# Sums of older slots behind the last ones, four more w_in chunks and two other w_out chunks converted in the attention, and g copied quarter by quarter

## The chip, the cores and the metric

The kernel runs on 1 core of one Trainium2 chip. The metric is the device time in microseconds (us): 574.38 is the median of 3 runs of the kernel before (573.75 to 574.51).

## The reference

Three layers stand one behind the other, all in fp32 (2304 tokens, width 512):

```python
q, k = rotate(q), rotate(k)                    # (4, 8, 576, 64)
attn = softmax(q @ k.T / 8)
x = (attn @ v)                                 # -> (2304, 512)

logits = x @ phi                               # soft MoE, 32 slots = 8 experts x 4
d = softmax over tokens of logits
slot_in = d.T @ x
slot_out[e] = relu(slot_in[e] @ w1[e]) @ w2[e] # 512 -> 1024 -> 512
x = (softmax over slots of logits) @ slot_out

h = x @ w_in                                   # 512 -> 2048
out = (h * sigmoid(h)) @ w_out                 # 2048 -> 512
```

## The kernel before

**Attention.** The 32 heads are worked as 16 pairs. A pair's loop is numbered in ticks (ten to a pair), and tables of numbers at the file's head say in which tick a side task is issued. Each pair rotates q and k (POOL, DVE, ACT), multiplies scores on PE (L353, L366), takes exponentials on ACT (L357) and multiplies by v on PE (L386). In between stand the soft MoE's logits and sums of batches 0 to 2.

**Side tasks in the attention.** w_in and w_out come as 64-bit words. `narrow` turns a 128x512 chunk into fp32 in three steps: one on ACT (L134) and two on DVE (L137, L140). `W_IN_AT` gives the ticks of 12 chunks of w_in (128 rows by 512 columns). Each is loaded by SP (0.5 MB), converted and stored to DRAM as fp32 (0.25 MB), to be read again later. `W_OUT_EARLY` names four chunks of w_out that are converted there and kept. The last four chunks of w_in are left for the last MLP (`load_last`, `conv_last`).

**Tail of the attention.** The last batch's slot sums are made in two halves, h0 and h1 (`half`). Each has logits, a maximum on DVE, an exponential on ACT (L533), small transposes (`d_t`, L550, L552), a copy to SBUF on DVE (L554) and the sums `sps` on PE (`s_mm`, L561, L565). `s_b` holds the sums of older tokens. `merge` (L568) adds h0's to it. `slots` then scales and adds h1's on DVE (L574) and folds the result to 32 slots, `si`, by a product with `stack_i` on PE (L580) and copies on DVE (L581), in two rounds. `lt` is the tokens' logits transposed, needed by the combine weights.

**Layers.** `layer1` (L871) and `layer2` (L892) are the experts' two products, on streamed weights. `slot_t` transposes a group's result to `so`.

**Last MLP.** The product `so` by w_in, called g, is 32 by 2048, and the combine weights times g give the hidden values. `g_product(n)` makes a quarter of g (512 columns) as a 128x128 tile of four pieces. For n = 1 to 3 `g_copy(n, r)` puts a piece r into the operand `gs` by four copies of 32x128, of which `ACT_QUADRANTS` says which go to ACT (L1103), the rest to DVE (L1105). `hidden(j, k)` makes step k of block j: products `hps` (L1049), sigmoid and products (L1053, L1056), and a split in high and low parts `ghi` and `glo` (L1059, L1062). In block 0 it also converts and splits a chunk of w_out (`split_wo`, `split_hl`: `wo_hi` on ACT L1031, `wo_lo` on POOL L1032). Then come 18 `ops` matmuls (L1154 to L1156), six groups of three. `G_STEPS` says behind which group of the 48 x 6 a side task is issued, such as a quarter's product, its copies, or a conversion.

What sets the order: inside `manual_schedule` (all up to `gs1`) the code's own order, engine by engine. Behind it a scheduler places the instructions in a similar order. Each engine works its queue in order. Tiles are tracked as wholes here, so a reader waits for all earlier writers of its tile.

## Time and profile before

| | |
|---|---|
| median of 3 runs | 574.38 us |
| the profiled execution's own time | 573.27 us |
| its span | 571.5 us |
| PE busy | 540.4 us (95%) |
| DVE busy | 316.9 us (55%) |
| ACT busy | 307.9 us (54%) |
| POOL busy | 111.3 us (19%) |
| attention loop | to about 282 |
| tail of the attention | 282 to 300.6 |
| layers | 300.6 to 338.2 |
| passage to the last MLP | 338.2 to 346.05 |
| last MLP with w_out's conversions | 346.05 to 401.5 |
| last MLP, the rest | 401.5 to 567.7 |

Times in the rows are in us from the span's start. PE is TensorE's matmul side, PEld its weight load, DVE VectorE, ACT ScalarE, POOL GpSimd, SP the queue that issues transfers. A row's bracket tells how long the engine had been idle before it, and what it waited for. An fp32 matmul shows as two records.

### The profile page before, as it was taken

The numbers are of one execution on the slowest core, as the hardware profiler recorded it, in microseconds if no ns is written. First come the engines' busy times: TensorE is split into PE (matmuls) and PEld (weight loads), VectorE is DVE, ScalarE is ACT, GpSimd is POOL, SyncE is SP. The second block draws the span as 40 slices with busy tenths as digits, with TensorE's granted clock in tenths as the row PEclk, the third lists the DMA queues.
The fourth block names the chain that finished last, engine by engine and source line by source line (L and its number), as shares of the span: only waits on it lengthen the run. The fifth ranks groups of instructions, "written<-read, shape, count | busy, mean of one in ns | idle before, by whom it ended". The sixth has DMA issues, their size and how long they took to land.

```text
span 571.5 us, 15141 instructions
## 1 busy us (share of the span) xinstructions
PE 540.4 (95%) x6219; PEld 438.1 (77%) x6219; DVE 316.9 (55%) x841; ACT 307.9 (54%) x612; POOL 111.3 (19%) x96
## 2 busy tenths in 40 slices
...
GB/s 301 95 56 206 266 244 278 203 116 172 224 231 172 207 265 166 249 166 107 296 322 382 306 359 179 135 93 75 0 93 18 1 1 1 96 16 0 2 0 111
DMA packets 36773, 88.70 MB, mean 155 GB/s; under 512 B 10560, under 2 KB 11872, under 8 KB 34784
## 3 DMA queue, kind: packets, MB, share of 16 engines
...
q10 hardware_dynamic: 10, 0.00, 0.0%
...
## 4 chain that ended last, share of the span: by engine, by line
PE 76%; ACT 10%; DVE 5%; DMA 4%; issue 3%; POOL 1%; SPq 1%; ACTq 0%; DVEq 0%
PE u L386 10%; PE ops L1156 10%; PE ops L1154 10%; PE ops L1155 10%; PE st L353 8%; PE psmx L300 3%; PE st_r L366 3%; PE l L871 3%; PE hps L1049 3%; ACT e L357 3%; PE xps L414 3%; DMA w_out_raw<-in_w_out_dram 2%; PE psmx L316 2%; ACT relu L308 2%; PE u L380 2%
## 5 line engine op out<-in xcount | busy, mean ns | idle before, releaser
L1056 DVE TENSOR_TENSOR hps<-hps,g 128x384 f32<-128x384 f32 x96 | 49.8, 561 | 84.6 <-ACT g L1053 84.3
L1053 ACT ACTIVATE g<-hps 128x384 f32<-128x384 f32 x96 | 42.3, 490 | 82.3 <-PE hps L1049 81.9
L1154 PE MATMUL ops<-wo_hi,ghi 128*128 128x512 f32 x216 | 84.7, 392 | 0.0
L1155 PE MATMUL ops<-wo_lo,ghi 128*128 128x512 f32 x216 | 84.4, 391 | 0.0
L1156 PE MATMUL ops<-wo_hi,glo 128*128 128x512 f32 x216 | 84.3, 390 | 0.0
L321 DVE CUSTOM_DVE_ANT_0 relu<-psmx,relu 128x288 f32<-128x288 f32 x140 | 57.7, 455 | 47.1 <-ACT e L357 36.3
L357 ACT ACTIVATE e<-st 128x512 f32<-128x512 f32 (+1 forms) x128 | 76.4, 650 | 10.9 <-PE st L353 10.9
L386 PE MATMUL u<-v,e 128*64 128x65 f32 x2048 | 80.6, 225 | 0.0
L386 PEld LDWEIGHTS u<-v,e 128*64 128x64 f32 x2048 | 71.5, 139 | 6.2 <-issue 3.0
L308 ACT ACTIVATE relu<-psmx 128x576 f32<-128x576 f32 x62 | 40.1, 652 | 51.7 <-PE psmx L300 33.6
L259 POOL TENSOR_TENSOR raw<-raw,tab 128x576 f32<-128x576 f32 x29 | 41.8, 1442 | 132.8 <-DMA raw<-in_qk_dram 96.7
L1062 DVE TENSOR_TENSOR glo<-hps,ghi 128x384 fp32r<-128x384 f32 x96 | 49.4, 552 | 5.0 <-ACT ghi L1059 1.8
L1059 ACT ACTIVATE ghi<-hps 128x384 fp32r<-128x384 f32 x96 | 45.6, 494 | 10.2 <-DVE hps L1056 10.1
L1156 PEld LDWEIGHTS ops<-wo_hi,glo 128*128 128x128 f32 x216 | 40.6, 188 | 8.5
L1155 PEld LDWEIGHTS ops<-wo_lo,ghi 128*128 128x128 f32 x216 | 40.6, 188 | 7.5 <-issue 0.4
L1154 PEld LDWEIGHTS ops<-wo_hi,ghi 128*128 128x128 f32 x216 | 40.6, 188 | 7.5 <-issue 0.2
L256 POOL TENSOR_TENSOR raw<-raw,tab 128x576 f32<-128x576 f32 x29 | 42.0, 1447 | 0.0
L353 PE MATMUL st<-hi 64*128 64x256 f32 (+1 forms) x256 | 39.7, 302 | 0.0
L353 PE MATMUL st<-mq,neg_a 64*128 64x256 f32 (+1 forms) x256 | 39.1, 297 | 0.6 <-DMA mq<-m 0.6
L353 PE MATMUL st<-hi,lo 64*128 64x256 f32 (+1 forms) x256 | 38.9, 296 | 0.0
L353 PE MATMUL st<-lo,hi 64*128 64x256 f32 (+1 forms) x256 | 38.9, 296 | 0.0
L397 DVE TENSOR_SCALAR r<-u 128x4 f32<-128x4 f32 (+1 forms) x32 | 5.2, 164 | 49.7 <-PE u L388 30.1
...
## 6 DMA issues: line engine op xcount, KB each, us to landing
...
```

The costliest lines, as they stand in the source:

```text
L308: act.activation(out=r, in_=pair[:, :, 0:HS], func=ACTF.Relu)
L321: dve.tensor_tensor_reduce(out=r[:, hd], in0=t[hd], in1=r[:, hd], scale=1.0, scalar=-3.0e38, op0=ALU.add, op1=ALU.max, accum_out=mxs[p % 2 ...
L353: pe.matmul(st[:, hd, 0:n], lhsT=a, rhs=b, start=i == 0, stop=i == 3, skip_group_check=True)
L357: act.activation(out=e[:, :, 0:n], in_=st[:, :, 0:n], func=ACTF.Exp, scale=0.125)
L386: pe.matmul(u[q:q + 64, 2 * i + hd], lhsT=e[:, hd, o:o + 64], rhs=x[:, hd], start=n == 0 and i + hd == 0, stop=n == 4, skip_group_check=True)
L1053: act.activation(out=g[i], in_=t[i], func=ACTF.Sigmoid)
L1056: dve.tensor_tensor(out=t[i], in0=t[i], in1=g[i], op=ALU.mult)
L1059: act.activation(out=ghi[:, i], in_=t[i], func=ACTF.Copy)
L1062: dve.tensor_tensor(out=glo[:, i], in0=t[i], in1=ghi[:, i].bitcast(F32), op=ALU.subtract)
L1154: pe.matmul(t, lhsT=a, rhs=wo_hi[k], start=k == 0, stop=False)
L1155: pe.matmul(t, lhsT=a, rhs=wo_lo[k], start=False, stop=False)
L1156: pe.matmul(t, lhsT=b, rhs=wo_hi[k], start=False, stop=k == 15)
```

## The change

1. `W_IN_AT` gets four more ticks (33, 63, 73, 103). All 16 chunks of w_in are converted in the attention, with a fourth fp32 tile in DRAM. `load_last` and `conv_last` go, and `load_in(3)` reads that tile back behind group 9 of the last MLP. The ACT step of the conversions writes one tile of two halves in turn.
2. `W_OUT_EARLY` is (0, 1, 6, 11) in place of (3, 6, 9, 12). The conversions of w_out 0 and 1 between the layers and the last MLP go. Their split (`wo_lo`) stays on DVE and stands ahead of `gs`.
3. Tail: `x_15(1)`, the transposes of the last x, stand behind the first of h1's logits. ACT no longer scales `s_b`; instead DVE makes `ss`, the 128x32 fold matrix times the scale. `merge` moves ahead of h1's copy L554. Five matmuls on constants are added (`busy`). `slots` copies h1's sums to SBUF (half on ACT, half on DVE) and folds older and last sums in PSUM by two groups of four matmuls, with one copy to `si`. `lt`'s transposes follow, and ACT copies them. The sum `den` is made last (`total`).
4. `slot_t` copies its 128x512 half on ACT, half on DVE.
5. `ACT_QUADRANTS` is (0, 1), and the copies of g's quarters are issued piece by piece, one piece behind the second `ops` group of each step. `G_STEPS` holds the three quarters' products. The first two `ops` groups of step 0 stand ahead of the rest of g's first quarter.

The diff, cut to its core:

```diff
@@ -39,21 +39,22 @@
-W_IN_AT = (17, 27, 37, 47, 53, 67, 77, 87, 93, 107, 117, 127)
+W_IN_AT = (17, 27, 33, 37, 47, 53, 63, 67, 73, 77, 87, 93, 103, 107, 117, 127)
...
-W_OUT_EARLY = (3, 6, 9, 12)
+W_OUT_EARLY = (0, 1, 6, 11)
...
-G_STEPS = (5, 7, 16, 19, 28, 14, 23, 37, 46, 53, 58)
-ACT_QUADRANTS = (0, 1, 2)
+G_STEPS = (5, 28, 52)
+LOAD_STEP = 9
+ACT_QUADRANTS = (0, 1)
@@ -90,7 +91,7 @@
-    w_in_32 = [dram.tile([128, 4, 512 if n else 384], F32, tag=f"w_in{n}", name=f"w_in_32_{n}") for n in range(3)]
+    w_in_32 = [dram.tile([128, 4, 512 if n else 384], F32, tag=f"w_in{n}", name=f"w_in_32_{n}") for n in range(4)]
@@ -163,17 +164,13 @@
-        elif n == 1:
+        elif n % 2:
...
-    def load_last(i):
-        t = raw_in[i] = rw.tile([128, 2, 1024], U32, tag=f"raw{1 - i}", name=f"w_in_raw3_{i}")
-        sp.dma_start(out=t, in_=w_in[256 * i:256 * i + 256, 3072:4096].rearrange("(k p) f -> p k f", p=128))
@@ -536,7 +533,8 @@
-                        act.activation(out=s_b[0][64:128], in_=s_b[0][64:128], func=ACTF.Copy, scale=sc[64:128, 5:6])
+                        ps["ss"] = p_r.tile([128, 3, NSLOT], F32, tag="dh0", name="ss")[:, 0]
+                        dve.tensor_scalar(out=ps["ss"], in0=stack_i[:, 0:NSLOT], scalar1=sc[:, 5:6], scalar2=None, op0=ALU.mult)
@@ -567,25 +565,24 @@
-                def slots():
-                    acc = s_b[0]
-                    for j in range(2):
-                        w = slice(256 * j, 256 * j + 256)
-                        dve.scalar_tensor_tensor(out=acc[0:64, w], in0=acc[0:64, w], scalar=sc[0:64, 5:6], in1=ps["s"][0:64, w], op0=ALU.mult, op1=ALU.add)
-                    t2 = ps_mx.tile([128, 2, 512], F32, tag="mx", name="si_ps")
-                    for j in range(2):
-                        t = t2[:, j]
-                        for k in range(2):
-                            c0 = 256 * j + 128 * k
-                            pe.matmul(t[:, NSLOT * k:NSLOT * k + NSLOT], lhsT=acc[:, c0:c0 + 128], rhs=stack_i[:, 0:NSLOT], start=True, stop=True)
-                        dve.tensor_copy(out=si[:, 2 * j:2 * j + 2], in_=t[:, 0:64].rearrange("p (k s) -> p k s", k=2))
+                def slots(t):
+                    o = hb[1][0:64, 0:DM]
+                    act.activation(out=o[:, 0:256], in_=ps["s"][0:64, 0:256], func=ACTF.Copy)
+                    dve.tensor_copy(out=o[:, 256:512], in_=ps["s"][0:64, 256:512])
+                    for k in range(4):
+                        pe.matmul(t[:, NSLOT * k:NSLOT * k + NSLOT], lhsT=s_b[0][:, 128 * k:128 * k + 128], rhs=ps["ss"], start=k == 0, stop=False, skip_group_check=True)
+                    for k in range(4):
+                        pe.matmul(t[:, NSLOT * k:NSLOT * k + NSLOT], lhsT=o[:, 128 * k:128 * k + 128], rhs=stack_i[0:64, 0:NSLOT], start=False, stop=True, skip_group_check=True)
+                    dve.tensor_copy(out=si, in_=t[:, 0:4 * NSLOT].rearrange("p (k s) -> p k s", k=4))
+                def total():
...
-                return logits, logits2, soft, expo, keep, d_t, s_mm, slots, merge
+                return logits, logits2, soft, expo, keep, d_t, s_mm, slots, merge, total
@@ -593,7 +590,7 @@
-            words, cv = {}, {}
+            words, cv, hws = {}, {}, []
@@ -608,7 +605,9 @@
-                cv[i] = (*narrow(words.pop(i), o, wa, f"hw{i}", f"w{NWA - 3}"), keep)
+                if not hws:
+                    hws.append(wa.tile([128, 2, 512], F32, tag=f"w{NWA - 3}", name="hw_in"))
+                cv[i] = (*narrow(words.pop(i), o, None, None, hw=hws[0][:, i % 2]), keep)
@@ -650,7 +649,7 @@
-            for i in range(12):
+            for i in range(16):
@@ -823,26 +822,35 @@
-            h1[0]((0, 1, 2))
+            h1[0]((0,))
+            x_15(1)
+            h1[0]((1, 2))
...
-            x_15(1)
...
+            h0[6]()
+            h0[8]()
+            t = ps_st.tile([128, 2, 512], F32, tag="st", name="lt3_ps")
+            def busy(n):
+                for _ in range(n):
+                    pe.matmul(t[0:64, 0, 256:512], lhsT=ones, rhs=cst_sb, start=True, stop=True)
+            busy(3)
+            h1[5]()
             h1[4]()
-            h0[6]()
-            h1[5]()
-            h0[8]()
+            busy(2)
             h1[6]()
-            t = ps_st.tile([128, 2, 512], F32, tag="st", name="lt3_ps")[:, 0]
+            h1[7](t[:, 1])
             for i, (o, n) in enumerate(CHUNKS[3]):
-                pe.transpose(t[0:n, NSLOT * i:NSLOT * i + NSLOT], hb[2][0:32, o:o + n], ident[0:32, 0:32])
-            h1[7]()
-            dve.tensor_copy(out=lt[:, 15:19], in_=t[:, 0:4 * NSLOT].rearrange("p (c s) -> p c s", c=4))
-            dve.tensor_copy(out=lt[0:64, 19], in_=t[0:64, 4 * NSLOT:5 * NSLOT])
+                pe.transpose(t[0:n, 0, NSLOT * i:NSLOT * i + NSLOT], hb[2][0:32, o:o + n], ident[0:32, 0:32])
+            act.activation(out=lt[:, 15:19], in_=t[:, 0, 0:4 * NSLOT].rearrange("p (c s) -> p c s", c=4), func=ACTF.Copy)
+            act.activation(out=lt[0:64, 19], in_=t[0:64, 0, 4 * NSLOT:5 * NSLOT], func=ACTF.Copy)
+            h1[9]()
@@ -899,7 +907,8 @@
-            act.activation(out=o, in_=op[g], func=ACTF.Copy)
+            act.activation(out=o[:, 0:256], in_=op[g][:, 0:256], func=ACTF.Copy)
+            dve.tensor_copy(out=o[:, 256:512], in_=op[g][:, 256:512])
@@ -968,13 +977,10 @@
-        load_wo(0)
         load_in(0)
-        load_wo(1)
...
-        load_last(0)
@@ -990,16 +996,10 @@
-            t, h = (wa.tile([128, 2, 512], F32, tag=f"w{i}", name=n) for i, n in ((3, "wf_first"), (4, "hw_first")))
-            for k in range(2):
-                first.append((t[:, k], narrow(raw_w.pop(k), t[:, k], None, None, hw=h[:, k])))
-        first = []
...
-        for f in first[0][1]:
-            f()
@@ -1072,13 +1072,6 @@
-    def conv_last(k):
-        if k % 2 == 0:
-            halves(3, k // 2)
-        words = raw_in[k // 2][:, k % 2].rearrange("p (n t) -> p n t", t=2)
-        for f in narrow(words, w_next[3, k], wa, f"hw3_{k}", "w3"):
-            f()
@@ -1112,13 +1105,25 @@
+    ops = {}
+    def products(j, k, i, ghi, glo):
+        if k == 0:
+            ops[j, i] = ps_o.tile([128, DM], F32, tag="o", name=f"ops{j}_{i}")
+        t = ops[j, i]
+        a, b = ghi[:, 128 * i:128 * i + 128], glo[:, 128 * i:128 * i + 128]
+        pe.matmul(t, lhsT=a, rhs=wo_hi[k], start=k == 0, stop=False)
+        pe.matmul(t, lhsT=a, rhs=wo_lo[k], start=False, stop=False)
+        pe.matmul(t, lhsT=b, rhs=wo_hi[k], start=False, stop=k == 15)
...
-        (wf0, _), (wf1, n1) = first
+        for k in range(2):
+            split_hl(k, wf_early[k], dve)
@@ -1126,34 +1131,29 @@
-        hidden(*seq[0], between=lambda: (split_hl(0, wf0, dve), g_product(0)))
-        n1[0]()
+        hidden(*seq[0], between=lambda: g_product(0))
+        for i in range(2):
+            products(0, 0, i, *gt[0, 0])
         g_spread()
-        for f in n1[1:]:
-            f()
-        split_hl(1, wf1, dve)
...
-    def copies(n):
+    extra = {}
+    def put(x, f):
+        extra.setdefault(divmod(x, NI), []).append(f)
+    put(LOAD_STEP, lambda: load_in(3))
+    for n, x in enumerate(G_STEPS):
+        put(x, lambda n=n: g_product(n + 1))
         for r in range(4):
-            g_copy(n, r)
-    extra = {}
-    for x, f in zip(G_STEPS, (lambda: g_product(1), lambda: copies(1), lambda: g_product(2), lambda: copies(2), lambda: load_last(1),
-                              lambda: conv_last(0), lambda: conv_last(1), lambda: conv_last(2), lambda: conv_last(3), lambda: g_product(3), lambda: copies(3))):
-        extra.setdefault(divmod(x, 6), []).append(f)
-    ops = {}
+            put(NI * (4 * n + r + 1) + 1, lambda n=n, r=r: g_copy(n + 1, r))
...
-            if k == 0:
-                ops[j, i] = ps_o.tile([128, DM], F32, tag="o", name=f"ops{j}_{i}")
+            if (j, k, i) not in ((0, 0, 0), (0, 0, 1)):
+                products(j, k, i, ghi, glo)
             t = ops[j, i]
-            a, b = ghi[:, 128 * i:128 * i + 128], glo[:, 128 * i:128 * i + 128]
-            pe.matmul(t, lhsT=a, rhs=wo_hi[k], start=k == 0, stop=False)
-            pe.matmul(t, lhsT=a, rhs=wo_lo[k], start=False, stop=False)
-            pe.matmul(t, lhsT=b, rhs=wo_hi[k], start=False, stop=k == 15)
```

How the rows move, at three places. A row is line, operation, output<-inputs with tile numbers, size, and a count where it repeats; all are one engine's, in the order of its queue.

The first place is the tail, from h1's transposes (`dps`) to the first product of the layers. DVE before:

```order
L554 COPY dh_4862<-dps_4911 128x96
L568 SCALAR_TENSOR_TENSOR s_b_77<-sps_4902,sc,s_b_77 64x512
L574 SCALAR_TENSOR_TENSOR s_b_77<-s_b_77,sc,sps_4918 64x256 x2
L581 COPY si<-si_ps 128x64 x2
L582 TENSOR_TENSOR scs<-sc,sb 128x2
L583 TENSOR_REDUCE den<-scs 128x1
L584 SCALAR_TENSOR_TENSOR den<-den,sc,sb 128x1
L585 TENSOR_SCALAR den<-den 128x1
L586 RECIPROCAL den<-den 128x1
L844 COPY lt<-lt_ps 128x128
L845 COPY lt<-lt_ps 64x32
```

DVE now:

```order
L537 TENSOR_SCALAR ss<-cst_sb,sc 128x32
L566 SCALAR_TENSOR_TENSOR s_b_77<-sps_4920,sc,s_b_77 64x512
L552 COPY dh_4880<-dps_4934 128x96
L571 COPY last_logits<-sps_4943 64x256
L576 COPY si<-lt_ps 128x128
L579 TENSOR_TENSOR scs<-sc,sb 128x2
L580 TENSOR_REDUCE den<-scs 128x1
L581 SCALAR_TENSOR_TENSOR den<-den,sc,sb 128x1
L582 TENSOR_SCALAR den<-den 128x1
L583 RECIPROCAL den<-den 128x1
```

PE before, from the same transposes (all `sps` products but the last are left out):

```order
L550 MATMUL dps_4911<-cst_sb,last_logits 128x32 x2
L552 MATMUL dps_4911<-cst_sb,last_logits 64x32 x2
...
L565 MATMUL sps_4918<-x_4751,dh_4862 32x64 x2
L842 MATMUL lt_ps<-cst_sb,last_logits 128x32 x4
L842 MATMUL lt_ps<-cst_sb,last_logits 64x32
L580 MATMUL si_ps<-cst_sb,s_b_77 128x32 x4
L871 MATMUL l_0_0_5037<-w_653,si 32x512
```

PE now:

```order
L841 MATMUL lt_ps<-cst_sb,ones 64x256 x3
L548 MATMUL dps_4934<-cst_sb,last_logits 128x32 x2
L550 MATMUL dps_4934<-cst_sb,last_logits 64x32 x2
L841 MATMUL lt_ps<-cst_sb,ones 64x256 x2
...
L563 MATMUL sps_4943<-x_4769,dh_4880 32x64 x2
L573 MATMUL lt_ps<-ss,s_b_77 128x32 x4
L575 MATMUL lt_ps<-cst_sb,last_logits 128x32 x4
L850 MATMUL lt_ps<-cst_sb,last_logits 128x32 x4
L850 MATMUL lt_ps<-cst_sb,last_logits 64x32
L879 MATMUL l_0_0_5063<-w_654,si 32x512
```

The fold matrix `ss` and the merge (now L566) stand ahead of h1's copy `dh` on DVE, five constant products (L841) stand on PE on both sides of h1's transposes, the two rounds of scaling, product and copy have become one, and the `lt` transposes stand behind the products.

The second place is the passage from the layers to the last MLP, on DVE, from the copy of the last group's `so` to the first hidden values. Before:

```order
L908 COPY so<-otp_5334 128x4x16
L137 TENSOR_SCALAR wf_first<-hw_first 128x512
L140 SCALAR_TENSOR_TENSOR wf_first<-w_out_raw_5212,wf_first 128x512
L929 TENSOR_TENSOR gs_5343<-g_ps,gs_5343 64x128
L1056 TENSOR_TENSOR hps_0_0_5397<-hps_0_0_5397,g_0_0_5401 128x384
L1056 TENSOR_TENSOR hps_0_1_5399<-hps_0_1_5399,g_0_1_5404 128x384
L1032 TENSOR_TENSOR wo_lo_5408<-wf_first,wo_hi_5407 128x512
L1062 TENSOR_TENSOR glo_0_5396<-hps_0_0_5397,ghi_0_5395 128x384
L1062 TENSOR_TENSOR glo_0_5396<-hps_0_1_5399,ghi_0_5395 128x384
L929 TENSOR_TENSOR gs_5343<-g_all,gs_5343 64x384
L137 TENSOR_SCALAR wf_first<-hw_first 128x512
```

Now:

```order
L911 COPY o_5351<-l_1_5259 128x256
L1032 TENSOR_TENSOR wo_lo_5389<-wf_early,wo_hi_5388 128x512
L917 COPY so<-otp_5354 128x4x16
L1032 TENSOR_TENSOR wo_lo_5393<-wf_early,wo_hi_5392 128x512
L938 TENSOR_TENSOR gs_5360<-g_ps,gs_5360 64x128
L1056 TENSOR_TENSOR hps_0_0_5424<-hps_0_0_5424,g_0_0_5428 128x384
L1056 TENSOR_TENSOR hps_0_1_5426<-hps_0_1_5426,g_0_1_5431 128x384
L1062 TENSOR_TENSOR glo_0_5423<-hps_0_0_5424,ghi_0_5422 128x384
L1062 TENSOR_TENSOR glo_0_5423<-hps_0_1_5426,ghi_0_5422 128x384
L138 TENSOR_SCALAR wf_5496<-hwo_5497 128x512
```

The two conversion steps ahead of `gs` (L929, now L938) are gone, as is the split between the products `hps` and `glo`; two splits of w_out (`wo_lo`, L1032) stand around `so`.

The third place is ACT in the last MLP's first steps, from the first half quarter `gh` of g. Before:

```order
L1095 ACTIVATE gh_5536<-g_ps_5519 128x128
L1103 ACTIVATE gs_5343<-gh_5536 32x128 x2
L1103 ACTIVATE gs_5343<-gl_5537 32x128
L1103 ACTIVATE gs_5343<-gh_5536 32x128 x2
L1103 ACTIVATE gs_5343<-gl_5537 32x128
L1103 ACTIVATE gs_5343<-gh_5536 32x128 x2
L1103 ACTIVATE gs_5343<-gl_5537 32x128
L1103 ACTIVATE gs_5343<-gh_5536 32x128 x2
L1103 ACTIVATE gs_5343<-gl_5537 32x128
L1053 ACTIVATE g_3_0_5573<-hps_3_0_5571 128x384
L1053 ACTIVATE g_3_1_5580<-hps_3_1_5578 128x384
```

Now:

```order
L1088 ACTIVATE gh_5552<-g_ps_5535 128x128
L1031 ACTIVATE wo_hi_5625<-wf_5620 128x512
L1096 ACTIVATE gs_5360<-gh_5552 32x128 x2
L1053 ACTIVATE g_3_0_5582<-hps_3_0_5580 128x384
L1053 ACTIVATE g_3_1_5589<-hps_3_1_5587 128x384
L1096 ACTIVATE gs_5360<-gh_5552 32x128 x3
L1059 ACTIVATE ghi_3_5578<-hps_3_0_5580 128x384
L1096 ACTIVATE gs_5360<-gh_5552 32x128
L1059 ACTIVATE ghi_3_5578<-hps_3_1_5587 128x384
L1031 ACTIVATE wo_hi_5674<-wf_5669 128x512
L1096 ACTIVATE gs_5360<-gh_5552 32x128
L1053 ACTIVATE g_4_0_5635<-hps_4_0_5633 128x384
```

Before, twelve copies stood in a row ahead of the next step's sigmoid; now eight stand in between the sigmoids and splits of two steps, and the others of this quarter are DVE's.

## Rows read from the trace of the kernel before

**Rows 1.** The page's first line: the span.

```profile
span 571.5 us, 15141 instructions
```

**Rows 2.** Windows by stage: start:end, length, busy per engine, TensorE clock, DMA share, GB/s.

```profile
301.44:304.85 3.41, 3.41 (x20) 1.08 (x16) 0.00 (x0) 0.00 (x0) 0.00 (x0) 0.50 1.05 399
338.20:346.05 7.85, 5.06 (x82) 3.75 (x83) 4.63 (x8) 5.55 (x13) 4.37 (x3) 1.00 0.43 174
346.05:401.50 55.45, 52.84 (x312) 41.20 (x311) 44.21 (x93) 44.98 (x109) 13.15 (x9) 1.00 0.37 124
401.50:567.70 166.20, 166.16 (x746) 138.75 (x746) 78.86 (x153) 71.43 (x155) 1.29 (x1) 1.00 0.06 24
```

**Rows 3.** Windows of five attention iterations, from one first L366 to the next.

```profile
173.35:190.71 17.36, 17.19 (x293) 15.12 (x293) 11.51 (x38) 11.83 (x22) 5.56 (x4) 1.00 0.41 134
239.47:256.86 17.39, 17.22 (x294) 15.14 (x293) 9.06 (x35) 10.97 (x21) 0.00 (x0) 1.00 0.60 193
141.79:156.93 15.14, 15.00 (x278) 13.58 (x277) 9.89 (x33) 10.22 (x19) 5.57 (x4) 1.00 0.67 230
207.21:222.36 15.15, 15.00 (x277) 13.57 (x277) 9.89 (x33) 10.81 (x20) 5.56 (x4) 1.00 0.57 196
222.36:239.47 17.11, 16.43 (x293) 14.03 (x293) 11.05 (x35) 10.67 (x20) 5.56 (x4) 1.00 0.75 262
```

**Rows 4.** Timeline of the tail: start, busy, engine, line, operation, tiles, count, idle before.

```profile
294.27 0.30 PE L550 MATMUL dps<-cst_sb,last_logits 32*128 32x32 f32 x2 [0.71 <-ACT last_logits L533]
...
295.03 0.73 DVE L568 SCALAR_TENSOR_TENSOR s_b<-sps,sc,s_b 64x512 f32<-64x512 f32 x1
...
295.17 1.07 PE L561 MATMUL sps<-x,dh 128*32 128x128 f32 x16 [0.36 <-DVE dh L554]
...
296.17 0.64 PE L565 MATMUL sps<-x,dh 64*32 64x64 f32 x16
...
296.91 0.87 DVE L574 SCALAR_TENSOR_TENSOR s_b<-s_b,sc,sps 64x256 f32<-64x256 f32 x2 [1.14 <-PE sps L565]
...
298.39 0.63 PE L580 MATMUL si_ps<-cst_sb,s_b 128*128 128x32 f32 x4 [0.32 <-DVE si L581]
...
300.60 1.92 PE L871 MATMUL l<-w,si 128*32 128x512 f32 x9 [1.58 <-DVE lt L845]
```

**Rows 5.** Timeline of the passage from the layers to the last MLP.

```profile
339.43 4.37 POOL L1032 TENSOR_TENSOR wo_lo<-wf_early,wo_hi 128x512 fp32r<-128x512 f32 x3 [22.65 <-DMA w_in<-w_in]
...
340.87 1.13 PE L1118 MATMUL warm<-cst_sb 128*128 128x256 f32 x4
...
341.02 1.64 DVE L140 SCALAR_TENSOR_TENSOR wf_first<-w_out_raw,wf_first 128x512 uint32<-128x512 uint32 x1
342.69 0.29 DVE L929 TENSOR_TENSOR gs<-g_ps,gs 64x128 fp32r<-64x128 f32 x1
...
343.04 0.61 PE L1049 MATMUL hps<-cs,gs 128*128 128x384 f32 x2 [1.04 <-DVE gs L929]
...
346.08 0.48 PE L1154 MATMUL ops<-wo_hi,ghi 128*128 128x512 f32 x1
```

**Rows 6.** The longest wait of PE, 338 to 402: total, times, longest.

```profile
PE hps L1049 <- DVE glo L1062: 1.8, 3, 1.2
```

**Rows 7.** Waits of SP's queue, 300 to 402.

```profile
SPq L176 <- PE g_all L1110: 14.2, 1, 14.2
```

**Rows 8.** Groups by line and form, 346 to 402: count, busy, mean ns, idle before.

```profile
L1103 ACT ACTIVATE gs<-gl 32x128 fp32r<-32x128 f32 x12 | 3.7, 308 | 1.2 <-DVE gl L1096 1.0
...
L140 DVE SCALAR_TENSOR_TENSOR w_in<-w_in_raw,w_in 128x512 uint32<-128x512 uint32 x4 | 2.7, 684 | 0.0
...
L134 ACT ACTIVATE hw<-w_in_raw 128x512 f32<-128x512 f32 x4 | 2.7, 682 | 0.0
...
L1105 DVE CAST gs<-gl 32x128 fp32r<-32x128 f32 x12 | 2.7, 222 | 0.2
...
L137 DVE TENSOR_SCALAR w_in<-hw 128x512 uint32<-128x512 uint32 x4 | 1.7, 419 | 0.0
```

2 lines of the change are left out of this document (1 added, 1 removed).

## The prediction

> **What bounds the kernel now.** I read the windows by stage first [rows 2]. From 401.5 on PE is busy for 166.16 of 166.20 us, and the change leaves that stretch alone: its length is fixed. So the time is decided by when this stretch begins, and by the idle time of PE ahead of it. Three stages show such time. In the first part of the last MLP PE is busy for 52.84 of 55.45 us, in the passage 5.06 of 7.85. The third is a loss that busy time hides: from 301.44 to 304.85 the granted clock is 0.50, the lower of the two levels (1.2 GHz), with all 3.41 us busy. Then I read the timeline of the tail [rows 4]: the last `sps` product ends at 296.81 (296.17 and 0.64), and the layers start at 300.60, after PE has idled for 1.58 us. The timeline of the passage [rows 5] shows DVE's conversion holding `gs`, and `gs` holding `hps`. The waits [rows 6] name DVE's `glo` as the longest hold on PE in the last MLP. Last I read five iterations of the attention [rows 3], where new work is put.
>
> The sum is made against the profiled execution, 573.27 us: its span of 571.5 [rows 1] and 1.77 around it. It lies 1.11 below the median of the runs, 574.38, so I add 1.11 at the end. About 0.2% (1.15 us) is what a measurement of this kernel can tell from no change.
>
> **The attention loop: four more conversions.** Each puts one step of 0.68 on ACT and two of 0.42 and 0.68 on DVE [rows 8], 1.79 in all, and on SP a load of 0.5 MB and a store of 0.25 MB. Iterations with and without such work can be compared. The one from 173.35 holds a conversion at a tick that ends in 3, as the four new ones do, and lasts 17.36. The one from 239.47 holds none and lasts 17.39, with 2.45 less on DVE and 0.86 less on ACT [rows 3]. The one from 207.21 has a w_out conversion beside its w_in one and lasts 15.15; the one from 141.79 has only the latter and lasts 15.14. In all four PE is busy for 99% of the time, so PE covers the conversions: price 0. Were that cover gone, the price would be PE's idle time of the worst iteration. From 222.36 on it lasts 17.11 with 16.43 busy, and conversion steps stand back to back with the rotary steps on DVE at its start; that makes 0.68 each, 2.7 for four. I take 0, with bounds 0 and +2.7. A gain is excluded, since nothing is taken out there. SP's transfers have room too: the DMA share is 0.41 to 0.75 in these iterations.
>
> **The tail.** Before, 3.79 us lie between the last `sps` and the layers: two scalings on DVE (0.87), two rounds of product (0.63 each) and copy, the steps of `den`, two copies of `lt`. Now there are two half copies of the sums. They share a tile, so the second waits for the first: 0.87 by the scalings of the same size. One group of four products counts 0.63, since the older sums' group runs under the copies. Then come one copy to `si` (0.3), the transposes of `lt` (0.5) and two copies on ACT (0.5), with hand-overs 0.35. That makes 3.15 and gains 0.64; `den` is off the path.
>
> Ahead of it something is lost. PE idled 0.71 ahead of h1's transposes and 0.36 ahead of `sps` [rows 4]. Two constant products took 1.13 at the passage [rows 5], so three make 1.3 to 1.7 and two 0.9 to 1.1. They fill those gaps and run over. DVE has the merge (0.73) ahead of `dh` now, but merges while PE runs the constants. The earlier transposes of x and logits of h1 give back some 0.5 of it. I take `sps` of h1 0.35 later (bounds -0.1 and +1.0). The tail gains 0.3 (bounds: 0.8 gained, 0.4 lost).
>
> **The clock at the layers' start.** At 0.50 the 3.41 us of products take twice what they need, so 1.7 is at stake. Before the fall PE had worked 0.63 and then idled 1.58. Now no single pause there is that long: product, copy (0.3), transposes, copies (0.5), then the layers. Five constants also lie in the 4 us ahead. I take it that the clock stays up: 1.7 gained (bounds 0 and 1.7).
>
> **The layers.** `slot_t`'s copy is split on two engines, but both halves write one tile, so they run one behind the other: 0, and 0.2 either way for the two groups. SP loses 2 loads of w_out and one of w_in here, which nothing in the layers waited for.
>
> **The passage.** Before, the conversion of w_out 0 stands on DVE to 342.66, the last step stretched to 1.64 where its usual length is 0.68 [rows 5, 8]. `gs` runs at 342.69, `hps` at 343.04, the first `ops` at 346.08. Now two splits (some 0.7 each) stand around the copy of `so`. The second runs beside the 32 products of g, so `gs` waits for these and for ACT alone: `hps` at 342.0 to 342.6, 0.4 to 1.0 earlier. A split and a conversion less also stand between `hps` and `ops`. But two `ops` groups now run ahead of the rest of g's first quarter, and the second step's `hps` waits for it, so PE has less in hand. I take 0.7 gained (bounds: 1.4 gained, 0.3 lost).
>
> While POOL ran its three splits (4.37 in all), DVE's step took 1.64. The Trainium skill, "SBUF — State Buffer", section "Who interferes with whom", says that a DVE instruction with two SBUF inputs and a GpSimd one that reads SBUF exclude each other, the second waiting for all of the first. The stretched step agrees. By that rule DVE's second split could wait out a POOL split, the passage would gain nothing, and the sum would be 570.4. I keep 0.7, since POOL has two splits left in place of three and 4.63 of 7.85 us of DVE were busy.
>
> **The last MLP to 401.5.** PE idles 2.61 us here [rows 2], 1.8 of it for `glo` [rows 6]. What held DVE and ACT goes: four conversions of w_in (ACT 2.7, DVE 1.7 and 2.7 [rows 8]) and ACT's runs of twelve copies, which stood ahead of the sigmoid. Twelve copies leave ACT (3.7) for DVE (2.7). ACT falls from 44.98 to 38.6 us, DVE from 44.21 to 42.5, so PE stays the bound. SP's queue no longer waits 14.2 us for g with w_out's loads behind it [rows 7]. I leave 0.6 of the idle time for the first two steps, where the lead is small: 2.0 gained (bounds 0 and 2.4).
>
> **Sum:** 0 - 0.3 - 1.7 - 0 - 0.7 - 2.0 = -4.7. So 568.6 by the profiled execution, and 569.7 with 1.11 added. With its own bounds this case reaches from 567.4 to 571.0.
>
> **Rivals.**
>
> *The clock falls all the same.* The last sums still pass through four hand-overs, in which PE works some 1.1 of 3 us. For it: the fall before came with PE working 1.3 of 3.8 us. Against it: the constants, and the passage, where PE idled 1.04 ahead of `hps` and kept the clock at 1.00 [rows 2, 5]. The Trainium skill, "TensorE: Matmul & The Clock Gate", section "A second HAM failure mode: psum-queue depth-cycling", says that short idle times between groups of products suffice to bring the clock down; by it this case would be the likely one. No run here shows which pause decides. The time is 1.7 more: 571.4. Chance 0.28.
>
> *PE goes on waiting in the last MLP.* DVE keeps 42.5 of 55 us, gets twelve more copies, and POOL's splits (13.15 us there) can meet its steps. If only 0.3 of the 2.61 goes, and nothing of the passage's 0.7, the sum is -2.3: 572.1. Against it: the chain there went through ACT's copies and conversions, which go. Chance 0.12.
>
> *Slower: the conversions stand in the iteration's path.* DVE and ACT then delay the rotary steps and the exponentials by the whole 1.79 of each, 7.2 for four, and the sum turns to +2.5: 576.9. The point from which this decides is 4.7 / 4, about 1.2 us for each. For it: the iteration of 17.11, with 0.68 lost. Against it: the pairs of equal iterations, and that none of the new ones adds a w_out conversion. Chance 0.09.
>
> **How the numbers follow.** The forecast has a chance of 0.51, the clock's rival 0.28, the waits' 0.12, the slower one 0.09. The predicted time is the forecast's, 569.7. The range starts at the forecast's lower bound, 567.4, takes in both middle rivals, and ends at 573.6, where the waits' rival with a fallen clock would lie (573.8). Faster by over 0.2% means below 573.2: the forecast, the clock's rival and most of the waits' one, 0.84. Within 0.2%: 0.07, mostly the waits' rival with the fall. Slower: 0.09.
>
> **What would show it.** Windows of the attention as long as before, each of the new conversions included. The layers' first products some 0.3 earlier, and no stretch at 0.50 behind them. The first `ops` some 0.7 earlier against the layers' end. PE's idle time between there and the steady stretch about 0.6 in place of 2.61, with no run of copies on ACT. The prediction is wrong if the iterations with the new conversions are longer, if the stretch at 0.50 is there again, or if `hps` still waits for `glo` or `gs` for more than 1 us in all.

## The result and the profile after

The changed kernel takes 580.78 us (median of 4 runs, 578.21 to 580.85), the kernel before 574.07 beside it (4 runs, 572.37 to 574.51): ratio 1.0111, 95% interval 1.008 to 1.0142. It is slower, and 569.7 was forecast.

The page of after: the span [rows 1], then busy time, share and instructions of each engine.

```profile
span 579.1 us, 15188 instructions
PE 547.1 (94%) x6237; PEld 440.1 (76%) x6237; DVE 327.9 (57%) x852; ACT 304.7 (53%) x602; POOL 113.4 (20%) x96
```

The profiled execution took 580.85 us. Its stages against those of before (the loop is the fifteen iterations from one first L366, now L363, to the next; the passage goes from ACT's last copy in `slot_t` to the first `ops`):

| stage | before | after | difference | forecast |
|---|---|---|---|---|
| up to the first iteration's mark | 26.29 | 24.15 | -2.14 | - |
| attention loop | 246.40 | 252.79 | +6.39 | 0 |
| tail | 27.91 | 28.48 | +0.57 | -0.3 |
| layers | 37.63 | 39.28 | +1.65 | 0, and -1.7 by the clock |
| passage | 7.85 | 6.01 | -1.84 | -0.7 |
| last MLP, first ops to last | 221.58 | 224.53 | +2.95 | -2.0 |

These sum to +7.6, the difference of the spans. The start varies between 24.1 and 26.3 from run to run, whatever the kernel (24.35 in h1_before_no_const, the kernel before less one product), so its -2.14 isn't the change's. Nor is the loop the same each time: in four more runs with this very loop and no fall of the clock in it (e4_no_busy, f1_no_const, f3_late_products, f4_act1) it took 252.38 to 254.18.

Windows of after: three iterations (the second and third answer to those from 141.79 and 207.21 in [rows 3]; the first, with a conversion where one stood before, took 17.36), the stretch at the lower clock, the passage and the first 55.45 us of the last MLP [rows 2].

```profile
106.57:124.00 17.43, 17.25 (x293) 15.15 (x293) 11.75 (x38) 11.79 (x22) 5.55 (x4) 1.00 0.51 171
140.49:158.02 17.53, 15.33 (x277) 13.65 (x277) 12.60 (x33) 10.71 (x20) 6.08 (x4) 1.00 0.62 204
209.79:226.66 16.87, 15.56 (x277) 13.69 (x277) 11.70 (x34) 10.71 (x20) 6.07 (x4) 1.00 0.67 223
306.16:309.57 3.41, 3.41 (x20) 0.85 (x16) 0.00 (x0) 0.00 (x0) 0.00 (x0) 0.50 0.96 341
344.70:350.71 6.01, 4.32 (x74) 2.92 (x74) 3.19 (x8) 4.30 (x11) 2.71 (x2) 1.00 0.37 147
350.71:406.16 55.45, 51.39 (x304) 39.69 (x304) 45.42 (x95) 41.12 (x95) 16.50 (x12) 1.00 0.31 105
```

The iteration from 140.49 took 15.14 before; now it is 17.53, with 2.2 us in which PE does nothing. The stretch at 0.50 is there again. The last MLP's 55.45 us hold 51.39 us of PE, less than before.

**The loop.** The timelines of SP, POOL and DVE around that iteration:

```profile
139.40 0.33 SPq L219 DMA_DIRECT2D raw<-in_qk_dram  x1
...
148.35 1.42 POOL L256 TENSOR_TENSOR raw<-raw,tab 128x576 f32<-128x576 f32 x1 [13.54 <-DMA raw<-in_qk_dram]
...
151.19 1.96 DVE L259 TENSOR_TENSOR raw<-raw 128x576 f32<-128x576 f32 x1
153.07 1.64 DVE L138 TENSOR_SCALAR w_in<-hw_in 128x512 uint32<-128x512 uint32 x1
154.74 0.69 DVE L141 SCALAR_TENSOR_TENSOR w_in<-w_in_raw,w_in 128x512 uint32<-128x512 uint32 x1
155.35 0.45 DVE L318 CUSTOM_DVE_ANT_0 relu<-psmx,relu 128x288 f32<-128x288 f32 x1
...
156.11 1.42 DVE L265 TENSOR_TENSOR lo<-raw,hi 128x576 fp32r<-128x576 f32 x2
```

The same rows before:

```profile
139.97 0.34 SPq L222 DMA_DIRECT2D raw<-in_qk_dram  x1
...
145.78 1.43 POOL L259 TENSOR_TENSOR raw<-raw,tab 128x576 f32<-128x576 f32 x1 [11.04 <-DMA raw<-in_qk_dram]
...
151.88 0.75 DVE L262 TENSOR_TENSOR raw<-raw 128x576 f32<-128x576 f32 x1
...
153.62 1.42 DVE L268 TENSOR_TENSOR lo<-raw,hi 128x576 fp32r<-128x576 f32 x2
```

And the waits of SP's and PE's queues in the loop of after:

```profile
SPq L219 <- DVE lo L265: 23.5, 10, 4.7
...
PE psmx L297 <- DVE mx L318: 1.9, 1, 1.9
```

Against the iteration's mark (141.79 before, 140.49 now), SP issues the raw load 1.09 ahead instead of 1.82, and POOL starts on its data 7.86 behind instead of 3.99. DVE's rotary step L259 then runs beside POOL's products and takes 1.96 in place of 0.75, the added L138 takes 1.64 in place of 0.42 [rows 8], and PE's next maximum waits for DVE. In DVE's queue the two added steps stand between the rotary step L259 and `lo` (L265). `lo` is the last reader of the raw buffer, SP's raw load L219 waits for it, and there are two such buffers, so a late `lo` makes the next raw load late: the next one goes out 0.43 ahead of its mark (157.59 and 158.02), where it was 1.82 (155.11 and 156.93).

The late issue is the smaller part of POOL's delay, 0.73 of 3.87 us. The rest is the load itself: from its issue to POOL's start it is 8.95 us (139.40 and 148.35), where it was 5.81 (139.97 and 145.78). Why the load takes longer was not isolated.

**The tail.** PE's and the copies' rows of after [rows 4]:

```profile
296.03 0.75 PE L511 MATMUL lgh<-xt,phi_sb 128*32 128x320 f32 x8
...
297.56 1.51 PE L841 MATMUL lt_ps<-cst_sb,ones 128*64 128x256 f32 x6
...
299.47 1.08 PE L841 MATMUL lt_ps<-cst_sb,ones 128*64 128x256 f32 x4
...
300.48 1.07 PE L559 MATMUL sps<-x,dh 128*32 128x128 f32 x16
...
301.48 0.64 PE L563 MATMUL sps<-x,dh 64*32 64x64 f32 x16
...
302.63 0.42 DVE L571 COPY last_logits<-sps 64x256 f32<-64x256 f32 x1 [2.79 <-ACT last_logits L570]
...
305.42 1.25 PE L879 MATMUL l<-w,si 128*32 128x512 f32 x8 [0.44 <-ACT lt L852]
```

From the end of `sps` (301.48 and 0.64) to the layers it is 3.30 us, where 3.79 were: 0.49 gained of the 0.64 forecast. DVE's copy L571 stands behind ACT's, as forecast, since they share a tile. Ahead of `sps` more was lost. It starts 4.45 behind h1's last logits (300.48 and 296.03), where it was 3.22 (295.17 and 291.95): the constants and the merge stand in that way. The earlier transposes and logits give 0.28 of these 1.23 back (from h1's first logits to its last it is 3.02 us in place of 3.30), so 0.95 is lost where I took 0.35.

**The layers.** PE in layer2's first group, after and then before:

```profile
325.17 1.93 PE L900 MATMUL l<-w,ht 128*32 128x512 f32 x12
327.03 0.70 PE L1122 MATMUL warm<-cst_sb 128*128 128x256 f32 x2
327.66 7.05 PE L900 MATMUL l<-w,ht 128*32 128x512 f32 x52
```

```profile
320.30 1.94 PE L892 MATMUL l<-w,ht 128*32 128x512 f32 x16
322.17 0.70 PE L1118 MATMUL warm<-cst_sb 128*128 128x256 f32 x2
322.80 5.41 PE L892 MATMUL l<-w,ht 128*32 128x512 f32 x48
```

The constant product that the program writes ahead of g's first quarter (`dummy(1)`) runs up here, some 20 us earlier: the code's own order, said ahead of the prediction to hold up to `gs1`, doesn't hold for it in either trace. Before it stood behind 16 records, four fours; now behind 12. The products go into four quarters of 32 columns, two products (four records) to a quarter in turn, and the quarters run side by side, four records in 0.43 us. With the constant between the third quarter's products and the fourth's, the first records go by threes, and the fourth quarter's rest is left over for the end. Windows of L900 alone in after, the last full one and the one behind it:

```profile
331.10:332.80 1.70, 1.70 (x20) 0.66 (x16) 1.00 1.04 404
332.80:334.50 1.70, 1.70 (x8) 0.33 (x3) 1.00 1.05 406
```

In the second, records start one by one, 0.43 apart, four in 1.72 us (four of its eight began in the first window).

**The passage** of after [rows 5]:

```profile
346.38 0.68 DVE L1032 TENSOR_TENSOR wo_lo<-wf_early,wo_hi 128x512 fp32r<-128x512 f32 x1
...
347.98 0.29 DVE L938 TENSOR_TENSOR gs<-g_ps,gs 64x128 fp32r<-64x128 f32 x1 [0.91 <-ACT gs L937]
...
348.33 0.83 PE L1049 MATMUL hps<-cs,gs 128*128 128x384 f32 x2
...
350.71 0.50 PE L1115 MATMUL ops<-wo_hi,ghi 128*128 128x512 f32 x1 [0.75 <-ACT ghi L1059]
```

DVE's second split keeps its 0.68 and is done long before `gs`, which waits for ACT: `hps` comes 3.62 behind the start of `slot_t`'s last copy on ACT, 1.19 earlier than before, and `ops` 2.38 behind `hps` instead of 3.04.

**The last MLP.** PE's waits in its first 60 us [rows 6], and two groups by line [rows 8]:

```profile
PE hps L1049 <- DVE glo L1062: 2.9, 3, 1.5
PE ops L1115 <- ACT ghi L1059: 0.9, 2, 0.8
PE hps L1049 <- DVE gl L1089: 0.8, 1, 0.8
```

```profile
L141 DVE SCALAR_TENSOR_TENSOR wf<-w_out_raw,wf 128x512 uint32<-128x512 uint32 x12 | 8.5, 706 | 0.3
L1098 DVE CAST gs<-gl 32x128 fp32r<-32x128 f32 x24 | 8.3, 344 | 0.4
```

Twelve conversions of w_out stand here, where ten and the rest of chunk 1's stood before, and a copy on DVE takes 344 ns where it took 222.

### The profile page after: what moved, and what is told of

It is laid out like the page before. It is cut to its first block, busy times and chain, and to the rows that moved or that the text cites. A ratio compares the mean times of both kernels' runs of the same rounds, so it can differ in the third digit from the quotient of the medians.

```text
span 579.1 us, 15188 instructions
## 1 busy us (share of the span) xinstructions
PE 547.1 (94%) x6237; PEld 440.1 (76%) x6237; DVE 327.9 (57%) x852; ACT 304.7 (53%) x602; POOL 113.4 (20%) x96
## 4 chain that ended last, share of the span: by engine, by line
PE 70%; DMA 9%; DVE 9%; ACT 7%; issue 4%; SPq 0%; ACTq 0%; POOL 0%; DVEq 0%
PE ops L1115 10%; PE ops L1116 10%; PE ops L1117 10%; PE u L383 9%; PE st L350 6%; DMA raw<-in_qk_dram 3%; PE psmx L297 3%; PE l L879 3%; PE hps L1049 3%; DMA w<-in_w_dram 2%; PE u L377 2%; PE st_r L363 2%; ACT e L354 2%; PE psmx L313 2%; DMA w_out_raw<-in_w_out_dram 2%
## 5 line engine op out<-in xcount | busy, mean ns | idle before, releaser
L256 POOL TENSOR_TENSOR raw<-raw,tab 128x576 f32<-128x576 f32 x29 | 42.0, 1447 | 134.6 <-DMA raw<-in_qk_dram 111.5
L253 POOL TENSOR_TENSOR raw<-raw,tab 128x576 f32<-128x576 f32 x29 | 44.8, 1545 | 0.0
```

What stands on the lines that cost most here:

```text
L253: eng.tensor_tensor(out=r[:, i, 0, w], in0=r[:, i, 0, w], in1=tab[:, 0, w], op=ALU.mult)
```

## The experiments

The loop's length is the first number of a window over its fifteen iterations; the other stages are cut as in the table above.

**Fewer conversions (e1_w12).** Twelve chunks in the attention, the last four loaded and converted in the last MLP, where the products of g's quarters also go back to 16 and 53:

```diff
-W_IN_AT = (17, 27, 33, 37, 47, 53, 63, 67, 73, 77, 87, 93, 103, 107, 117, 127)
+W_IN_AT = (17, 27, 37, 47, 53, 67, 77, 87, 93, 107, 117, 127)
...
-G_STEPS = (5, 28, 52)
+G_STEPS = (5, 16, 53)
...
+        load_last(0)
...
+    put(28, lambda: load_last(1))
+    for k, x in enumerate((14, 23, 37, 46)):
+        put(x, lambda k=k: conv_last(k))
```

> The changed kernel with only the first part undone: 12 chunks of w_in in the attention, the last four loaded and converted in the last MLP as before (at steps 14, 23, 37 and 46 of the 48 x 6). The changed kernel's trace has 6.4 us more in the attention's iterations (2.4, 1.3 and 1.7 of it in those from the eighth, ninth and twelfth first L363). Theory A, the four chunks cost this: the iterations go back to the lengths of before within 0.2 each, and the time falls by some 6 us, less what four conversions cost in the last MLP (0 to 2): 575 to 577. Rival, the iterations are longer for another reason (the other w_out chunks' loads, or a different start): they stay long, and the time stays at 580 or rises.

579.26 us against 573.96, ratio 1.0081 (1.0051 to 1.0111). The loop is 247.07, so its loss is the added conversions'. But the time fell by 1.5 only, to above the 575 to 577 expected: in the profiled execution the last MLP went to 227.22, with a fall of the clock in it, and the layers to 40.36, with a longer one.

**Transfers alone, steps alone (e2_traffic, e3_compute).** The one leaves out the added chunks' steps on ACT and DVE: they are loaded, and the stores send an older chunk. The other leaves out their loads: the steps work on words that are there already, and the stores come at tick 133.

```diff
...
+                if i in ADDED:
...
+                    cv[i] = [lambda: None] * 3 + [store]
+                    return
```

```diff
+                if i in ADDED:
+                    words[i] = last[-1]
+                    return
...
-                cv[i] = (*narrow(words.pop(i), o, None, None, hw=hws[0][:, i % 2]), keep)
+                cv[i] = (*narrow(words.pop(i), o, None, None, hw=hws[0][:, i % 2]), (lambda: None) if i in ADDED else keep)
...
+            at(133, late_stores)
```

> The changed kernel with the four added chunks of w_in loaded and stored as there, but without their steps on ACT and DVE (the store sends an older chunk, so these columns of w_in are not the real ones). Theory A1, the traffic: the load of 0.5 MB and the stores stand beside the load of q and k (1152 KB), which lands later (8.8 us behind its issue in place of some 5.8 in the iteration from 140.5 on), so POOL's rotary steps start later and meet DVE's steps: the three long iterations stay within 0.5 of the changed kernel (17.5, 17.7, 16.9). Theory A2, the steps on ACT and DVE: the three go back to 15.1, 16.4 and 15.2. Both together: part of the way.

> The changed kernel with the four added chunks' steps on ACT and DVE, but without their loads (the steps convert the words of the chunk before once more) and with their stores put off to tick 133 (so these columns of w_in are not the real ones). Theory A1, the traffic: the iterations go back to 15.1, 16.4 and 15.2 within 0.2. Theory A2, the steps: they stay at 17.5, 17.7 and 16.9. Both together: part of the way.

One run each: 574.31 and 577.52 us. Windows over the loop of before, e2_traffic, e3_compute and after:

```profile
26.29:272.69 246.40, 241.51 (x4308) 213.53 (x4308) 153.56 (x495) 160.89 (x287) 73.68 (x53) 0.98 0.59 195
```

```profile
24.38:270.76 246.38, 241.45 (x4308) 213.37 (x4308) 156.53 (x496) 161.09 (x287) 75.93 (x54) 0.98 0.64 208
```

```profile
24.34:273.60 249.26, 242.74 (x4308) 213.84 (x4308) 159.12 (x504) 163.33 (x291) 74.61 (x54) 0.98 0.59 197
```

```profile
24.15:276.94 252.79, 243.25 (x4308) 213.93 (x4308) 163.90 (x504) 163.23 (x291) 76.97 (x54) 0.98 0.62 203
```

Transfers alone cost nothing, steps alone 2.9, both 6.4, so neither of the two theories holds alone. DVE's column shows why it is more than the sum: four conversions are 4.4 us of DVE by [rows 8], but its busy time grows by 3.0 with the transfers alone, by 5.6 with the steps alone and by 10.3 with both. The steps delay `lo` and with it the issue of the raw loads: the one for the iteration that answers to 140.49 goes out 1.10 ahead of its mark in e3_compute, 1.82 in e2_traffic. The transfers make such loads slower: from issue to POOL's start it is 7.4 to 8.5 us in six iterations of e2_traffic, at most 7.1 before. Both bring POOL's work beside DVE's, and DVE's rows stretch.

**Other places (e5_place, g1_place2, h2_13).** The new lines stand in this order; the last is in g2_mend, below, 13 in place of 33.

```diff
-W_IN_AT = (17, 27, 33, 37, 47, 53, 63, 67, 73, 77, 87, 93, 103, 107, 117, 127)
+W_IN_AT = (17, 27, 37, 47, 53, 57, 63, 67, 77, 87, 93, 97, 103, 107, 117, 127)
+W_IN_AT = (7, 17, 27, 33, 37, 47, 53, 57, 67, 77, 87, 93, 97, 107, 117, 127)
+W_IN_AT = (7, 13, 17, 27, 37, 47, 53, 57, 67, 77, 87, 93, 97, 107, 117, 127)
```

> The changed kernel with 16 chunks of w_in as there, two of the four added ones at other ticks: 57 and 97 in place of 33 and 73. These two lie in the iterations with the soft MoE's work, where PE needs 17.4 us whatever DVE does. Theory A3 (from the two runs before: the traffic alone costs 0, the steps alone 2.9, both 6.4): a step costs where DVE's queue has a rotary step ahead of it and a relu that PE waits for behind it, and a delay there frees the buffer of q and k later, so the next load and POOL's rotary steps come later too. Then the place decides: the iterations' sum falls from 252.8 to 246.5 to 248.5, and the time by 4 to 6 us, to 575 to 577. Rival, the number decides (16 chunks are more than DVE, SP and the loads carry): the sum stays above 251.

> The changed kernel with the four added conversions at ticks 7, 33, 57 and 97 in place of 33, 63, 73 and 103; at 7, 57 and 97 DVE's two steps fall at a tick that ends in 1, where no lo of the rotary step waits behind them. Place theory: what costs is DVE's steps just ahead of lo, which frees the buffer of the next raw load; then the fifteen iterations sum to 246.8 to 248.5 (246.40 before, 252.79 after, 249.97 with two of them moved). Load theory: any four conversions more on DVE cost about 1.5 each, wherever they stand: 251.5 or more.

> The kernel of g2_mend with a conversion at tick 13 in place of 33. In g2_mend the iterations 3 to 5, behind tick 33, are 0.3, 0.6 and 1.0 longer than before. Place theory: at 13, where the raw loads still run ahead, DVE's steps hold no load; iterations 3 to 5 come back to 15.9, 16.4 and 17.4, the loop to 246.9 to 248, and the time falls by 1 to 2 against g2_mend (570.4): 568.5 to 569.5. If not, the loop stays at 248.5 or more and the time at 570 or more.

e5_place: 578.77 us against 573.33 (ratio 1.0097, 1.008 to 1.0114), loop 249.97, between what the place theory (at most 248.5) and its rival (over 251) expected. g1_place2: 575.11 in one run, loop:

```profile
24.54:272.85 248.31, 242.38 (x4309) 213.91 (x4309) 159.96 (x504) 163.44 (x291) 74.84 (x53) 0.98 0.62 206
```

The same sixteen conversions cost 1.9 in place of 6.4, by their ticks alone (1.7 and 2.7 with the same ticks in g3_tail and g2_mend, below). The iteration that took 17.53 is 15.15 again, with a conversion at the ticks it always had. That is the place theory, within its bounds; what is left stands in the iterations behind tick 7 (0.8) and 33 (1.0). h2_13 missed its 568.5 to 569.5: 574.66 against 573.83 (ratio 0.9996, 0.9974 to 1.0018), loop 249.99. At 13 the loss moved into the third and fourth iterations (16.40 and 17.22, where 15.14 and 15.86 were), so the places early in the loop are not free either. How late each `lo` may come was not measured.

**The constants in the tail (e4_no_busy).**

```diff
-            busy(3)
...
-            busy(2)
```

> The changed kernel without the five constant products of the tail. In its trace they hold h1's transposes 0.65 and the products sps another 0.6 us back, and the clock falls to 0.5 behind them all the same for some 3.4 us. Theory B, they are pure delay: the layers' first product comes 1.0 to 1.3 us earlier against the start of h1's logits, the fall is as long as before, and the time falls by 1 (the weights' later release stays). Rival, they shorten the fall: without them the stretch at 0.5 is longer by 1 us or more, or starts earlier in the tail, and the time stays within 0.3.

581.89 us (580.12 to 583.12), ratio 1.013 (1.01 to 1.016). The window at the lower clock in the profiled execution, 583.12:

```profile
300.51:310.75 10.24, 9.41 (x69) 6.47 (x67) 1.47 (x7) 0.73 (x3) 0.00 (x0) 0.50 0.63 216
```

Without the constants h1's `sps` starts 3.59 behind the last logits (300.21 and 296.62), so they cost 0.86 there. But the clock is low for 10.24 us in place of 3.41, and the tail is 1.77 longer. In this execution they would pay for themselves, and they don't keep the clock up. The times don't settle it: two of the four executions have a mean granted clock of 0.982 and 0.985, no lower than after's, so the long fall isn't in them, and the intervals of the two ratios overlap.

**The fold matrix in `si`'s tile (e8_ss).**

```diff
-                        ps["ss"] = p_r.tile([128, 3, NSLOT], F32, tag="dh0", name="ss")[:, 0]
+                        ps["ss"] = si[:, 0]
```

> The changed kernel with the scaled fold matrix ss kept in the tile of si, in place of a tile of the attention's space. Theory W: the last five weight loads ahead of the layers wait for that space, with ss until the products of the older sums have read it; they were issued 2.27 ahead of the layers' start (3.75 before), and the layers took 39.3 us (37.6 before), the products of layer 2 running one by one as their weights land. Then the loads are issued some 1 us earlier and the layers take 38.0 to 38.6. Rival: the loads wait for h1's sums or something else behind them anyway, or the layers are longer for another reason: 39.3 within 0.3.

583.62 us in one run. The layers are 37.66, below the 38.0 to 38.6 expected, and for another reason: the constant stands behind 16 records again. Why it moves was not settled. The loop was 256.81, with a fall of the clock in it.

**No constant in the layers (f1_no_const; h1_before_no_const in the kernel before).**

```diff
-        dummy(1)
```

> The changed kernel without the one constant product (the first of the three on constants in the passage) that stands in the layers between the third and the fourth of the four 32-column products of layer2. Theory: behind it the fourth quarter of the array runs one product behind the other three, and at the end of that group four products run one by one: 1.72 us. Then the layers (first product to the copy of the second group's sums) go from 39.28 to about 37.6 us, and everything else stays. Rival 1, the weights come late (SP issues them 1 us later than before): 39.3 stays. Rival 2, only the constant's own time: 39.28 less 0.2 to 0.35, 39.0.

> The kernel before, without the one constant product in its layers, which stands there at a boundary of four products (1.20 us from the product ahead of it to the one behind, where 0.43 is usual). If a full-width product between 32-column products costs 0.75 at a boundary, the layers go from 37.63 to 36.9 (35.2 where the clock doesn't fall), and the time by 0.75, 572.5 against 573.2. If PE only waits there for something else that the constant covers, the layers stay at 37.6.

578.49 us in one run, and 571.62 against 573.83 for the kernel before (ratio 0.997, 0.9955 to 0.9986). PE in f1_no_const:

```profile
325.22 7.14 PE L900 MATMUL l<-w,ht 128*32 128x512 f32 x64
```

All 64 records come in fours. The layers take 35.19, less than the 37.6 expected, since in this execution the clock didn't fall there. g1_place2 and e6_act3, also without a fall there, have the constant where after has it, and take 37.59. So the constant costs 2.40, and after's 39.28 less 37.59 is the fall's price, 1.69. In the kernel before, at a boundary of four, it cost 37.63 less 36.85, 0.78. So 1.6 of the 2.40 is the fourth quarter's lone run. The weights, whose last loads SP issues 2.26 us ahead of the layers in place of 3.75, hold nothing here. The time of h1_before_no_const fell by more than these 0.78, and part of that is the clock's: its mean is 0.979 in one of 12 executions, in 15 of the 23 of the kernel before.

**The last MLP (e6_act3, e7_early, f2_row, f4_act1, f3_late_products).**

The edits in this order:

```diff
-ACT_QUADRANTS = (0, 1)
+ACT_QUADRANTS = (0, 1, 2)
```

```diff
-W_OUT_EARLY = (0, 1, 6, 11)
+W_OUT_EARLY = (0, 1, 3, 5)
```

```diff
-G_STEPS = (5, 28, 52)
+G_STEPS = (5, 16, 53)
+C_STEPS = (7, 19, 58)
...
-            put(NI * (4 * n + r + 1) + 1, lambda n=n, r=r: g_copy(n + 1, r))
+            put(C_STEPS[n], lambda n=n, r=r: g_copy(n + 1, r))
```

```diff
-ACT_QUADRANTS = (0, 1)
+ACT_QUADRANTS = (0,)
```

```diff
-        for i in range(2):
-            products(0, 0, i, *gt[0, 0])
...
-            if (j, k, i) not in ((0, 0, 0), (0, 0, 1)):
-                products(j, k, i, ghi, glo)
+            products(j, k, i, ghi, glo)
```

> The changed kernel with three of g's four quadrants copied by ACT, as before, piece by piece as in the change. In the last MLP the changed kernel needs 224.5 from the first ops to the end, 2.95 more than before, with 4.6 of waits for DVE and ACT. Theory M1, the twelve copies that went to DVE (2.7 us, and 0.5 to 0.9 more where POOL's splits run) hold glo: the stretch falls to 222.5 to 223.3. Rival M2, the denser w_out conversions of the first steps hold it: it stays at 224.5 within 0.4, or rises as ACT gets 3.7 us more.

> The changed kernel with w_out chunks 0, 1, 3 and 5 converted early in place of 0, 1, 6 and 11. Steps 2 to 5 of the last MLP then convert two chunks in place of four. Theory M2, the conversions of four steps in a row make DVE and ACT late there: from the first ops to the end 222.5 to 223.5 in place of 224.5. Rival M1, the copies of g do it: 224.5 within 0.4. The attention is as in the changed kernel.

> The changed kernel with the copies of each quarter of g in a row, behind groups 7, 19 and 58, and the products at 5, 16 and 53, as before. Theory 1: copies piece by piece write the one tile of gs between the steps, so each next hps product waits for the copies just issued; in a row the stretch from the first ops to the end goes from 224.5 to about 222.5. Theory 2: ACT and DVE are full with the conversions, and where the copies stand changes nothing: 224.5 within 0.4. Theory 3: a row of copies holds the sigmoid of the next step, worse than now: 225.5 or more.

> The changed kernel with one quadrant of the copies on ACT and three on DVE (12 copies more on DVE, 12 less on ACT). Moving 12 to ACT cost 2.7 us. Theory 1, ACT's queue holds the sigmoid and with it PE: the stretch from the first ops to the end falls from 224.5 to 223 or less. Theory 2, DVE's queue is the one that holds (PE's waits name glo and gl): 225.5 or more. Theory 3, neither: 224.5 within 0.4.

> The changed kernel with the first two groups of products behind g's first quarter again, as before. Theory 1: the two early groups stand ahead of g_all and so of step 1's hps, and the hidden values lose lead that they never make up, since ACT and DVE are nearly full; without them the stretch from the first hps to the end goes from 226.9 (2.38 and 224.53) to about 225.2 (224.62 before). Theory 2: the early groups gain what they were put there for; without them the stretch grows to 227.3 or more. Theory 3: neither, 226.9 within 0.3.

One run each: 584.51, 587.19, 583.78, 582.93 and 579.80 us; what counts is the stretch from the first `ops`, 224.53 in after. More copies on ACT: 227.21, so M1 fails. Other chunks early: 226.31, which neither theory expected. Copies in a row: 223.76, so 0.8 of the loss at most. Fewer copies on ACT: 224.48, nothing. Without the early products: 221.24, and with the 0.6 by which `ops` then starts later, 224.22 from the first `hps` against 226.91, better than the 225.2 expected. PE's waits in f3_late_products, and its window that answers to the one above:

```profile
PE hps L1049 <- DVE glo L1062: 2.8, 3, 1.4
PE g_all L1103 <- ACT gf L1085: 0.5, 1, 0.5
```

```profile
352.95:408.40 55.45, 52.58 (x312) 41.68 (x312) 45.01 (x97) 41.29 (x97) 16.76 (x12) 1.00 0.32 105
```

The early groups put `g_all` 4.01 us behind the first `hps` in place of 2.10, and with it step 1's `hps` 6.29 (354.62 and 348.33) in place of 4.69 (354.66 and 349.97). The steps then start 0.6, 0.7, 1.8 and 2.5 later against the first `hps` (steps 1 to 4): a lead once lost grows, since DVE is busy for 45 of 55 us.

**All three undone (g2_mend), with the old tail (g3_tail), and the passage alone (g4_twelve).** g2_mend takes the places of g1_place2 and leaves out `dummy(1)` and the early products; g3_tail also puts back the old `slots` and order of the tail; g4_twelve is g3_tail with twelve chunks in the attention and the quarters' products at 16 and 53, as e1_w12 has them.

```diff
-W_IN_AT = (17, 27, 33, 37, 47, 53, 63, 67, 73, 77, 87, 93, 103, 107, 117, 127)
+W_IN_AT = (7, 17, 27, 33, 37, 47, 53, 57, 67, 77, 87, 93, 97, 107, 117, 127)
...
-        dummy(1)
...
-        for i in range(2):
-            products(0, 0, i, *gt[0, 0])
...
```

> The same places, and without the constant product in the layers and without the two early groups of products. If the three findings add up: the layers 37.6 less 0.75 (the constant at a group's boundary costs 0.75), so 36.9 with a clock fall of 3.41 there and 35.2 without; from the first hps to the end 224.2; the time against before: loop +0.4 to +2, tail +0.6, layers -0.75, to the first hps -1.2, from there -0.4: 0.2% to 0.3% faster at best, 573 to 575. If they don't add up, over 576.

> The kernel of g2_mend with the tail of the attention as it was before (two scalings, two rounds, no constants). If the new tail is worth 0.6 less than the old one, as the stretch from the last mark to the layers says (28.48 against 27.91), this is 0.6 faster than g2_mend: 572.5 to 574.5. If the constants keep the clock's fall short, as the run without them said (10.24 us of fall), it is 1 to 3 us slower than g2_mend.

> The kernel before with only the passage's part of the change (w_out 0 and 1 converted in the attention, slot_t's copy on two engines, g's quarters piece by piece), the last four chunks of w_in left to the last MLP, the old tail, no early products, no constant in the layers. Expected: loop 246.4 to 247.1, tail 27.9, layers 36.9, to the first hps 3.62, from there to the end 224.2 to 225.5 (224.62 before): 1.0 to 2.5 us faster than before, 571.6 to 573. If the conversions in the last MLP cost more than 2 there, no faster.

Twelve runs each, against 573.23 (29 runs): g2_mend 570.37 us, ratio 0.9956 (0.9931 to 0.998); g3_tail 571.96, 0.9962 (0.9944 to 0.9981); g4_twelve 574.26, 1.0016 (1.0 to 1.0033). So the three findings account for the loss, and g2_mend is 0.4% faster than the kernel before, more than expected; g4_twelve is no faster, where 571.6 to 573 was expected. The traced execution of g2_mend is one of its slowest (573.53, of 568.36 to 573.81), so its stages don't show the gain. The intervals of new and old tail overlap. By its stages the new one is 0.3 longer here (28.18 and 27.91), but its mean granted clock is 0.985, the value of the executions without a fall, in 4 of 12 runs (old tail: 2 of 12; before: 2 of 29). In g4_twelve the last MLP takes 226.08 where g3_tail takes 221.61: leaving w_in's four conversions there, with the products moved for them, costs 4.5.

## Why the prediction was wrong, step by step

**The attention loop, forecast 0 (bounds 0 and +2.7), measured +6.39: the step that failed.** "In all four PE is busy for 99% of the time, so PE covers the conversions: price 0." The equal pairs of [rows 3] don't carry that. The short ones, 15.14 and 15.15, are not one with and one without: DVE has 33 instructions and 9.89 us in both, and the trace shows one conversion's two steps in each, behind `lo` (w_out's in the one from 207.21; the w_in steps named beside it fall, on DVE, into the next iteration). The long ones, 17.36 and 17.39, do compare, and the one from 173.35 even has DVE's two steps between the rotary step and `lo`:

```profile
184.72 0.75 DVE L262 TENSOR_TENSOR raw<-raw 128x576 f32<-128x576 f32 x1
185.38 0.42 DVE L137 TENSOR_SCALAR w_in<-hw 128x512 uint32<-128x512 uint32 x1
185.84 0.69 DVE L140 SCALAR_TENSOR_TENSOR w_in<-w_in_raw,w_in 128x512 uint32<-128x512 uint32 x1
...
187.73 1.41 DVE L268 TENSOR_TENSOR lo<-raw,hi 128x576 fp32r<-128x576 f32 x2
```

But there PE has 17.2 us of work with or without a conversion. No pair told what the same order costs in a shorter iteration, or in two in a row: the one ahead of 140.49 has it too and keeps its length (16.49, and 16.47 before), but its next raw load goes out late, and the one from 140.49, with an added conversion of its own, pays 2.39. PE's share says that PE is the bound, not how much slack the chain behind it has, from raw load over POOL and DVE back to the free buffer; the bound of 0.68 each took the delay to stay in its iteration. The slower rival, 7.2 for four conversions, came near in size. Its way was another: not the rotary steps and exponentials themselves, but the buffer that is freed late and the loads that land late. The argument set against it, the equal pairs, was the mistake.

**The tail, forecast -0.3, measured +0.57.** The part behind `sps` gained 0.49 (0.64 forecast); ahead of it 0.95 was lost, within the bound of 1.0 but not the 0.35 that I took. The constants alone cost 0.86 (e4_no_busy).

**The clock, forecast -1.7, measured 0.** The rival came true: the stretch at 0.50 is as long as before. What it costs was sized right (1.69). The rule of the Trainium skill quoted for this rival ("TensorE: Matmul & The Clock Gate", section "A second HAM failure mode: psum-queue depth-cycling") agrees with after's trace, where no pause ahead of the fall is as long as the 1.58 us of before. But g1_place2, f1_no_const and e6_act3, with the same tail and the same pauses (0.38 and 0.44), had no fall there, so those pauses don't decide alone; what does was not settled.

**The layers, forecast 0, measured +1.65.** The term was put at nothing because only `slot_t` of the change's text stands there, and I didn't look at the order there. The constant had moved by four records, 1.6 us by f1_no_const against h1_before_no_const.

**The passage, forecast -0.7 (bounds -1.4 and +0.3), measured -1.84.** Right in its mechanism, too small: step by step, 1.19 to `hps`, where 0.4 to 1.0 stood, and 0.66 from there. The rival's collision on POOL didn't come; DVE's split kept 0.68. The Trainium skill's rule on the two ("SBUF — State Buffer", section "Who interferes with whom") shows in the loop instead, where DVE's L259, with two SBUF inputs, took 1.96 beside POOL's products and 0.75 before.

**The last MLP, forecast -2.0 (bounds 0 and -2.4), measured +2.95.** Two steps failed. I took four conversions of w_in out, and forgot that the two w_out chunks that leave the passage for the attention put two others back here: 12 conversions in the steps instead of 10. ACT has 41.12 us where 38.6 was forecast, DVE 45.42 where 42.5 was. And the early products, for which I left 0.6 of idle time, cost 2.7 (f3_late_products). Without them the stretch from the first `hps` gains 0.4 against before (224.22 and 224.62), not 2.0. What keeps the other 1.6 was not isolated; PE still waits 2.8 us for `glo` there, where it was 1.8.

**The range.** It didn't follow from the terms either. The stages' own bounds sum to 567.9 and 578.0, and the range was 567.4 to 573.6; 580.78 lies outside both.
